# Gated linear attention and a maxout block on one core: a third unit in two-token rows, padded log sums without padding, and new due times in the kernel's planner

## Chip, cores and metric

One Trainium2 chip, one core. The metric is the device time of one execution in microseconds (us), the median over several runs. Lower is better.

## What is computed

For each of 4 batches and 8 heads a recurrent state of 48 x 48 is decayed and updated over 768 tokens, and read out by q. The result (3072 tokens x 384 features) goes through two projections whose maximum is projected back.

```python
for t in range(S):                                   # q, k, v, alpha: (4, 8, 768, 48)
    state = alpha[:, :, t, :, None] * state + einsum('bhd,bhe->bhde', k[:, :, t], v[:, :, t])
    y[:, :, t] = einsum('bhd,bhde->bhe', q[:, :, t], state)
x = y.transpose(0, 2, 1, 3).reshape(B * S, H * D)    # 3072 x 384
out = maximum(x @ w1, x @ w2) @ w_out                # d_ff = 1024
```

## The kernel before, in words

**Units.** The work is cut into 12 units of 256 tokens: unit u is batch u % 4, token block u // 4. A unit has two chunks of 128 tokens. Each unit passes two stages, `gla(u)` (the recurrence, in chunk form) and `moe(u)` (the two projections and the output).

**The recurrence of a unit.** ACT takes the logarithm of alpha (`ln`, L463). PE sums the logarithms along the tokens with a triangular matrix (`sums`, `e_cs`: L474 or L480) and adds up the whole unit for the decay between chunks (L506). From unit 2 on (`PAIR`), POOL first adds the two halves into the tile `ls` (L498), and L506 works on that. ACT makes the exponentials (L511, L513, L516). POOL multiplies k (L552) and DVE q (L554) with them; PE transposes both (L562), DVE copies them out of PSUM (L565 or L570). PE makes the scores (L653), DVE masks them (L675), PE multiplies with v and the carried state (L684, L687), ACT copies the result (L695), PE transposes it (L701), DVE copies it (L706 or L710) into `xt`. The state goes through PE (L624, or L581), ACT or DVE (L636 to L640) and POOL (L605, L611).

**The projections of a unit.** The maximum is written as x w2 + relu(x (w1 - w2)), so the weights are prepared once: DVE makes `w12` = w1 - w2 (L442), PE, DVE and ACT make w2 w_out (L415 to L436), ACT or POOL cast w_out (L447). Per unit PE does h = x w12 (L741, four pieces of six matmuls), ACT or DVE the relu (L752, L749), PE the output product (L772: three matmuls on `w2o` and `xt`, eight on `wo` and `gt`, for each of two halves), ACT the copy (L780), and an ACT queue the store (L788).

**Two-token rows.** `TWO` lists the units whose q, k and v are loaded as rows of two neighbouring tokens (384 B per head and row) instead of one (192 B). alpha is always loaded so. Such a unit has three loads of 384 KB for q, k, v (L384); another has six of 192 KB (L398). In a unit of `TWO`, the sums use the whole PE array (`ti`, `ts`, L474); otherwise they use 64 rows of it (`t2`, L480), which the code calls tiled. `v` is brought into place by two POOL copies (L536) and two ACT copies (L540) instead of two POOL copies `vc` (L573), the state product is one L581 group of 16 matmuls instead of two L624 groups of 4, and L653 of either chunk needs the transposes of both.

**What sets the order.** All instructions are first listed with an engine, an assumed duration, an assumed latency to the reader, the tiles read and written, and a key. `Plan.schedule` then walks through time: each engine takes, of what is ready by the assumed times and has its PSUM banks, the step with the lowest key; after a tiled step on PE the `join` key counts instead, which for L480 is 10u - 5 and for L653 lower by 50. The order found is written out per engine; on the chip an engine runs its instructions in exactly that order and waits for what is late. `gla(u)` has keys 10u to about 10u + 5, `moe(u)` 10u + 20 to 10u + 26. `OFF0` adds 8.8 to the key of PE's output products of units 0 and 1 and -0.7 to that of POOL's `kn` (L552) there. Loads stand in SP's order; their assumed latency grows from 2.5 to 5.0 us (`LATE`) with the unit. Where the plan leaves PE idle in its first 40 us, `busy` puts matmuls on zeros (L453).

**Loads.** Seven buffers (`NLD`) take the units in turn; the weights first lie in buffers 4 to 6. `HEAD` is the order of the first loads: units 0 and 1 and the weights. Then unit 2 and so on follow.

Of the kernel before, what the change touches and what calls it, by code (L numbers as in the profile page):

```python
# [23 lines left out]
class Plan:  # L24
# [16 lines left out]
        self.psum.setdefault(name, [banks, group, 0, None])  # L41

    def add(self, eng, fn, dur, reads=(), writes=(), key=0.0, lat=None, ps=(), tiled=False, join=None):
        if self.u is not None and writes and isinstance(writes[0], tuple):
            d = (self.off0 if self.u < 2 else self.off).get(f"{eng}:{writes[0][0]}", 0)
            key, join = key + d, None if join is None else join + d
        o = Op(len(self.ops), eng, fn, dur, self.LAT[eng] + self.PAD if lat is None else lat, key)
        o.tiled, o.join = tiled, key if join is None else join
        for r in reads:
            if r in self.last_w:  # L50
                o.deps.add(self.last_w[r])
            self.readers.setdefault(r, []).append(o.n)
        for w in writes:
            if w in self.last_w:
                o.deps.add(self.last_w[w])
            for r in self.readers.pop(w, ()):
                if r != o.n:
                    o.deps.add(r)
            self.last_w[w] = o.n
        for x in (*reads, *writes, *ps):  # L60
            if x in self.psum and x not in o.ps:
                o.ps.append(x)
                self.psum[x][2] += 1
        o.w = (*writes, *reads)[:1]
        self.ops.append(o)
        return o
# [127 lines left out]
RELU_DVE = 1  # L194
TM_ACT = 1
X_LAST = 0
LATE = 2.5
KEY_T2 = 17
TWO = (0, 1)
MERGE = 3  # L200
COMBO = 99
JOIN_CS = -5
# [2 lines left out]
RING = 3  # L205
PAIR = 2
PAIR_ON = 'POOL'
OFF = {}
OFF0 = {'PE:op': 8.8, 'POOL:kn': -0.7}
HEAD = 'k0 a0 a1 q0 v0 k1 q1 w20 w22 w21 wo0 v1 wo1 wo2 wo3 w11 w10 w13 w12'  # L210


# [1 line left out]
def kernel(  # L214
# [75 lines left out]
        return t.rearrange("p (h r d) -> p r h d", r=2, h=H)  # L290

    P = Plan()
    P.off, P.off0, P.u = OFF, OFF0, None
    add = P.add

    def bank(x):
# [73 lines left out]
    for i in range(RING):  # L370
        add("DVE", lambda i=i: nc.vector.memset(KN[i], 0.0), 0.2, writes=[("kn", i)], key=-6)
        add("DVE", lambda i=i: nc.vector.memset(QN[i], 0.0), 0.2, writes=[("qn", i)], key=-5)
    for i in range(4):
        add("DVE", lambda i=i: nc.vector.memset(SB[i], 0.0), 0.2, writes=[("sb", i)], key=-4)


    def load(u, what="akqv"):
        n, (b, cp) = u % NLD, (u % B, u // B)
        t0 = 256 * cp
        lat = 2.5 + max(0.0, min(LATE, LATE * (u - 1) / 3.0))  # L380
        ws = [({4: "w2f", 5: "w1f", 6: "wof"}[u], g) for g in range(3 if u == 4 else 4)] if u in (4, 5, 6) else []

        def pairs(dst, src, keys):
            add("SP", lambda: nc.sync.dma_start(  # L384
                out=dst.rearrange("p (h x) -> p h x", h=H),
                in_=src[b, :, t0 : t0 + 256, :].rearrange("h (p r) d -> p h (r d)", r=2)),
                1.26 if u in TWO else 1.5, writes=[*keys, *ws], key=-1, lat=lat)

        if "a" in what:
            pairs(LD[n][:, 0, :], alpha, [("af", n)])  # L390
        rest = [x for x in (("k", "kf", KF, k), ("q", "qf", QF, q), ("v", "vf", VF, v)) if x[0] in what]
        if u in TWO:
            for _, nm, T, src in rest:
                pairs(T[n], src, [(nm, n, 0), (nm, n, 1)])
            return
        for a in range(2):
            for _, nm, T, src in rest:
                add("SP", lambda T=T, src=src, a=a: nc.sync.dma_start(  # L398
                    out=nat(T[n])[:, a],
                    in_=src[b, :, t0 + 128 * a : t0 + 128 * a + 128, :].rearrange("h p d -> p h d")),  # L400
                    0.99, writes=[(nm, n, a), *ws], key=-1, lat=lat)


    def load_w(m, g):
        fs = slice(256 * g, 256 * g + 256)
        if m == "2":
            dst, src, t = w2f[:, g, :], moe_w2[128 * g : 128 * g + 128, :], 1.36
        elif m == "1":
            dst, src, t = w1f[:, :, fs], moe_w1[:, fs].rearrange("(s p) f -> p s f", p=128), 1.15
        else:  # L410
            dst, src, t = wof[:, 2 * g : 2 * g + 2, :], moe_w_out[fs, :].rearrange("(s p) d -> p s d", p=128), 1.1
        add("SP", lambda: nc.sync.dma_start(out=dst, in_=src), t, writes=[(f"w{m}f", g)], key=-1, lat=2.5)

    def w2_rows(ds):
        add("ACT", lambda: nc.scalar.copy(out=w2h[:, ds, :], in_=w2f[:, ds, :]),  # L415
# [52 lines left out]

    def e_cs(u):
        lg = LG[u % 2]  # L470
        if u in TWO:
            for i in range(2):
                for r in range(2):
                    nc.tensor.matmul(csv(u, i), lhsT=ts if r > i else ti, rhs=lg[:, r, :, 0:D],  # L474
                                     start=(r == 0), stop=(r == 1))
            return
        for r in range(2):
            for a in range(2):
                s = slice(64 * a, 64 * a + 64)
                nc.tensor.matmul(csv(u, a), lhsT=t2[s, r, 128 * a : 128 * a + 128], rhs=lg[s, r, :, 0:D],  # L480
                                 start=(r == 0), stop=(r == 1))

    def sums(u):
        by2 = u in TWO
        add("PE", lambda: e_cs(u), 0.65 if by2 else 0.33, reads=[("lg", u % 2), "tt" if by2 else "t2"],
            writes=[("cs", u, 0), ("cs", u, 1)], key=10 * u + (0 if by2 else CS_UP), tiled=not by2, join=10 * u + (0 if by2 else JOIN_CS))

    def exps(u):
        lg, de, k0 = LG[u % 2], DE[u % 8], 10 * u
# [5 lines left out]
        ls = LS[u % 2]  # L495
        if pair:
            ns = nc.vector if PAIR_ON == "DVE" else nc.gpsimd
            add(PAIR_ON, lambda: ns.tensor_add(out=ls, in0=lg[:, 0], in1=lg[:, 1]),  # L498
                0.35 if PAIR_ON == "DVE" else 0.6, reads=[("lg", u % 2)], writes=[("ls", u % 2)], key=k0)

        def e_de():
            for j in range(HP):
# [16 lines left out]
    def gla(u):  # L519
# [10 lines left out]
        if by2:  # L530
            vx, qu = VX[TWO.index(u)], QU[TWO.index(u) % 2]
            vk = ("vx", u)
            v2 = two(VF[n])
            for a in range(2):
                s = slice(64 * a, 64 * a + 64)
                add("POOL", lambda a=a, s=s: nc.gpsimd.tensor_copy(out=vx[s, a : a + 2], in_=v2[s]),  # L536
                    0.9, reads=[("vf", n, a)], writes=[(vk, a)], key=k0 + 2.2)
            for a in range(2):
                o = slice(64 - 64 * a, 128 - 64 * a)
                add("ACT", lambda a=a, o=o: nc.scalar.copy(  # L540
                    out=vx[o, 2 * a], in_=v2[64 * a : 64 * a + 64, 1 - a]),
                    0.5, reads=[("vf", n, a)], writes=[(vk, 2 + a)], key=k0 + 2.5)

        def prep(i):
# [4 lines left out]
            qin = two(QF[n])[:, i] if by2 else nat(QF[n])[:, i]  # L549
            rk = [("kf", n, x) for x in ((0, 1) if by2 else (i,))]  # L550
            rq = [("qf", n, x) for x in ((0, 1) if by2 else (i,))]
            add("POOL", lambda: nc.gpsimd.tensor_mul(out=kn[:, :, 0:D], in0=kin, in1=EM[m3]),  # L552
                0.95, reads=[*rk, ("em", m3)], writes=[("kn", m3)], key=kk)
            add("DVE", lambda: nc.vector.tensor_mul(out=qn[:, :, 0:D], in0=qin, in1=csv(u, i)),  # L554
                0.5, reads=[*rq, ("cs", u, i)], writes=[("qn", m3)], key=kk)
            tp = ("tp", u, i)
# [7 lines left out]
            if by2:  # L564
                add("DVE", lambda: nc.vector.tensor_copy(  # L565
                    out=qu[:, :, :, :, i, :].rearrange("p a w j c -> p (w j) a c"),
                    in_=b16(tp, 1024).rearrange("p (y a c) -> p y a c", a=2, c=64)),
                    0.65, reads=[tp], writes=[("qu", u, i)], key=kk)
            else:
                add("DVE", lambda: nc.vector.tensor_copy(  # L570
                    out=QK[m3], in_=b16(tp, 1024).rearrange("p (w j c) -> p w j c", w=2, j=HP)),
                    0.6, reads=[tp], writes=[("qk", m3)], key=kk)
                add("POOL", lambda: nc.gpsimd.tensor_copy(out=VC[ci % 4], in_=nat(VF[n])[:, i]),  # L573
                    0.48, reads=[("vf", n, i)], writes=[("vc", ci % 4)], key=kk)
# [12 lines left out]
        def chunk(a):  # L587
# [6 lines left out]
                P.ps(x, 1, "g")  # L594
            if by2:
                qt = [qu[:, a, w].rearrange("p j r c -> p j (r c)") for w in range(2)]
                rqk, vc, rv, um, ru = [("qu", u, 0), ("qu", u, 1)], vx[:, 2 * a], [(vk, x) for x in range(4)], u2, "u2"
            else:
                qt = [QK[m3][:, w] for w in range(2)]
                rqk, vc, rv, um, ru = [("qk", m3)], VC[m4], [("vc", m4)], u16, "u16"  # L600
# [56 lines left out]
            elif a == 0:  # L657
                for x in (("pp", u, 1, 0), ("pp", u, 1, 1)):
                    P.ps(x, 1, "g")
                rd = [("qk", (2 * u + x) % RING) for x in range(2)]  # L660
                wr = [*pp, ("pp", u, 1, 0), ("pp", u, 1, 1)]
                if u >= COMBO and u + 1 < NU:
                    P.u = u + 1
# [198 lines left out]
```

## Time and profile before

| | |
|---|---|
| Time, median of 3 runs | 138.80 us (138.77 to 138.87) |
| The profiled execution | 139.23 us, its span 137.5 us |
| PE busy | 132.1 us (96%) |
| DVE, ACT, POOL busy | 95.6, 80.4, 77.3 us |
| L453 (matmuls on zeros) | 132 pieces, 11.0 us |
| L480 / L474 | 40 / 8 matmuls |
| L498 (POOL, `ls`) | 10 of 1153 ns |
| L536, L573 (POOL, v) | 4 of 820 ns, 20 of 502 ns |
| Loads L384 of k, q, v | 2 each, 384 KB |
| Loads L398 of k, q, v | 20 each, 192 KB |
| PE clock granted | full throughout |

The span is the time from the first to the last instruction of the profiled execution; its own time is 1.73 us longer, and the profiled execution is 0.43 us above the median of the runs. Durations below come from the profiled execution. PE is TensorE's matmuls, PEld its weight loads, DVE VectorE, ACT ScalarE, POOL GpSimd, SP SyncE; SPq and ACTq are DMA queues issued there. A matmul's own duration includes its pipeline, so the time between starts, or the rows of the chain of waits, tell what it costs PE.

### The profile page before, as it was taken

The numbers are of one execution on the slowest core, as the hardware profiler recorded it, in microseconds if no ns is written. First come the engines' busy times: TensorE is split into PE (matmuls) and PEld (weight loads), VectorE is DVE, ScalarE is ACT, GpSimd is POOL, SyncE is SP. The second block draws the span as 40 slices with busy tenths as digits, with TensorE's granted clock in tenths as the row PEclk, the third lists the DMA queues.
The fourth block names the chain that finished last, engine by engine and source line by source line (L and its number), as shares of the span: only waits on it lengthen the run. The fifth ranks groups of instructions, "written<-read, shape, count | busy, mean of one in ns | idle before, by whom it ended". The sixth has DMA issues, their size and how long they took to land.

```text
span 137.5 us, 4265 instructions
## 1 busy us (share of the span) xinstructions
PE 132.1 (96%) x1671; PEld 102.1 (74%) x1671; DVE 95.6 (70%) x202; ACT 80.4 (58%) x172; POOL 77.3 (56%) x138
## 2 busy tenths in 40 slices
PE   6999699999999999999999999999999999999991
PEld 6889586886667768777777877877777778787870
DVE  4948879953868967878977859858839748574300
ACT  3294790878355585575754944937837539245341
POOL 7469339317548548688685864973966928300000
PEclk9999999999999999999999999999999999999999
DMA  3999999899998997999999989999989630030213
GB/s 92 325 325 402 373 377 349 227 188 236 221 280 189 280 240 153 286 218 200 277 184 205 293 165 225 232 184 302 210 194 290 127 117 0 5 114 0 82 37 114
DMA packets 87428, 28.59 MB, mean 208 GB/s; under 512 B 81520, under 2 KB 86768, under 8 KB 87408
## 3 DMA queue, kind: packets, MB, share of 16 engines
q1 hardware_dynamic: 84240, 23.60, 72.8%
q10 hardware_dynamic: 3168, 4.72, 9.1%
q8 instruction: 13, 0.21, 0.6%
q14 instruction: 7, 0.06, 0.2%
HBM read 23.59 MB, written 4.72 MB: 206 GB/s over the span
## 4 chain that ended last, share of the span: by engine, by line
PE 85%; SPq 5%; DMA 5%; ACT 2%; issue 1%; ACTq 0%
PE pb L772 31%; PE pb L741 23%; PE pb L562 7%; SPq L384 5%; DMA ld<-in_moe_w_dram 5%; PE pb L653 5%; PE pb L687 3%; PE pb L432 3%; PE pb L701 3%; PE pb L684 3%; PE pb L480 3%; PE pb L624 2%; PE pb L506 1%; PE pb L422 1%; ACT w2h L415 1%
## 5 line engine op out<-in xcount | busy, mean ns | idle before, releaser
L772 PE MATMUL pb<-wo,gt 128*128 128x384 f16 (+2 forms) x200 | 38.9, 319 | 0.0
L552 POOL TENSOR_TENSOR kn<-ld,em 128x384 f16<-128x384 f32 x24 | 23.5, 998 | 21.4 <-ACT em L511 18.8
L741 PE MATMUL pb<-xt,w 128*128 128x256 f16 x288 | 35.4, 272 | 0.0
L675 DVE TENSOR_TENSOR pt<-pb,u 128x512 f16<-128x512 f32 x48 | 29.9, 683 | 0.9 <-PE pb L653 0.6
L741 PEld LDWEIGHTS <-w 128*128 128x128 f16 x288 | 27.0, 98 | 3.6
L752 ACT ACTIVATE gt<-pb 128x512 f16<-128x512 f32 x37 | 21.8, 604 | 11.8 <-PE pb L741 11.4
L611 POOL TENSOR_TENSOR sb<-tm,dd 64x192 f16<-64x192 f32 x40 | 20.8, 520 | 7.0 <-DVE tm L636 3.1
L780 ACT COPY os<-pb 128x384 f32<-128x384 f32 (+2 forms) x25 | 11.6, 468 | 19.8 <-PE pb L772 19.7
L772 PEld LDWEIGHTS <-gt 128*128 128x128 f16 x200 | 17.2, 97 | 7.6
L570 DVE COPY qk<-pb 128x1024 f16<-128x1024 f16 x20 | 13.7, 687 | 9.3 <-PE pb L562 6.1
L498 POOL TENSOR_TENSOR ls<-lg 128x512 f16<-128x512 f16 x10 | 11.5, 1153 | 8.8 <-ACT lg L463 8.3
L772 PE MATMUL pb<-w2o,xt 128*128 128x384 f16 (+2 forms) x75 | 15.8, 320 | 0.0
L511 ACT ACTIVATE em<-pb 128x384 f32<-128x384 f32 x24 | 10.8, 489 | 8.5 <-PE pb L480 8.5
L554 DVE TENSOR_TENSOR qn<-ld,pb 128x384 f16<-128x384 f32 x24 | 12.3, 549 | 4.5 <-ACT pb L513 3.9
L695 ACT CAST yc<-pb 128x384 f16<-128x384 f32 x24 | 11.9, 498 | 2.7 <-PE pb L687 2.7
L710 DVE COPY xt<-pb 128x384 f16<-128x384 f16 x20 | 7.1, 354 | 9.0 <-PE pb L701 6.9
L463 ACT ACTIVATE lg<-ld 128x768 f16<-128x768 f32 x12 | 10.3, 854 | 3.8 <-DMA ld<-in_alpha_dram 3.8
L749 DVE TENSOR_SCALAR gt<-pb 128x512 f16<-128x512 f32 x11 | 7.6, 692 | 6.7 <-PE pb L741 6.4
L453 PE MATMUL pb<-wsrc 128*128 128x128 f16 x132 | 11.0, 249 | 1.1 <-DVE wsrc L307 1.1
L636 DVE TENSOR_TENSOR tm<-pb,sb 64x192 f32<-64x192 f32 x32 | 11.3, 352 | 0.6
L687 PEld LDWEIGHTS <-pt 128*128 128x128 f16 x192 | 9.6, 96 | 1.9 <-DVE pt L675 0.3
L453 PEld LDWEIGHTS <-wsrc 128*128 128x128 f16 x132 | 9.8, 115 | 1.2 <-DVE wsrc L307 1.1
(81 smaller groups left out, 193.2 us busy)
## 6 DMA issues: line engine op xcount, KB each, us to landing
ld<-in_alpha_dram SPq DMA_DIRECT2D x12, 384.0 KB, 5.2
out_dram<-os ACTq DMA_DIRECT2D x11, 384.0 KB, 4.0
ld<-in_k_dram SPq DMA_DIRECT2D x20, 192.0 KB, 4.8
ld<-in_q_dram SPq DMA_DIRECT2D x20, 192.0 KB, 4.6
ld<-in_v_dram SPq DMA_DIRECT2D x20, 192.0 KB, 4.3
ld<-in_moe_w_dram SPq DMA_DIRECT2D x3, 512.0 KB, 6.7
ld<-in_moe_w_out_dram SPq DMA_DIRECT2D x4, 384.0 KB, 8.0
ld<-in_moe_w_dram SPq DMA_DIRECT2D x4, 384.0 KB, 8.0
```

The costliest lines, as they stand in the source:

```text
L453: nc.tensor.matmul(PB[b][:, 0:128], lhsT=wsrc, rhs=wsrc, start=True, stop=True)
L552: add("POOL", lambda: nc.gpsimd.tensor_mul(out=kn[:, :, 0:D], in0=kin, in1=EM[m3]), 0.95, reads=[*rk, ("em", m3)], writes=[("kn", m3)], ke ...
L554: add("DVE", lambda: nc.vector.tensor_mul(out=qn[:, :, 0:D], in0=qin, in1=csv(u, i)), 0.5, reads=[*rq, ("cs", u, i)], writes=[("qn", m3)], ...
L570: add("DVE", lambda: nc.vector.tensor_copy(out=QK[m3], in_=b16(tp, 1024).rearrange("p (w j c) -> p w j c", w=2, j=HP)), 0.6, reads=[tp], w ...
L611: add("POOL", lambda r=r, e=e: nc.gpsimd.tensor_mul(out=sb[r, :, e], in0=TM[tmo][r], in1=dd[r, :].unsqueeze(2).to_broadcast([64, HP, D])), ...
L675: add("DVE", lambda e=e: nc.vector.tensor_mul(out=pt[:, e], in0=b32(pp[e], 512).rearrange("p (j c) -> p j c", j=HP), in1=uv.unsqueeze(1).t ...
L687: nc.tensor.matmul(t[:, 96 * j + D * e : 96 * j + D * e + D], lhsT=pt[:, e, j, :], rhs=vc[:, 2 * j + e, :], start=not has, stop=(e == 1) o ...
L695: add("ACT", lambda: nc.scalar.copy(out=yc, in_=b32(yp, DM)), 0.38, reads=[yp], writes=[("yc", ci % 2)], key=kk)
L741: nc.tensor.matmul(t[:, m, :], lhsT=w12[:, ds, f * 128 : f * 128 + 128], rhs=xt[:, ds].rearrange("p a c -> p (a c)"), start=(ds == 0), sto ...
L752: add("ACT", lambda g2=g2, v2=v2: nc.scalar.activation(out=g2, in_=v2(), func=ACTF.Relu), 0.48, reads=[x], writes=[("gt", u % 3, f2)], key ...
L772: nc.tensor.matmul(b32(x, c1 - c0), lhsT=l, rhs=r, start=first and y == 0, stop=last and y == len(ws) - 1)
L780: add("ACT", lambda m=m, x=x, c0=c0, c1=c1: nc.scalar.copy(out=os_[:, m, c0:c1], in_=b32(x, c1 - c0)), 0.06 + w / 1200.0, reads=[x], write ...
```

## The change

- **Unit 2 joins `TWO`**, with a third pair of `VX` tiles and the two `QU` tiles used in turn; its output rows are stored accordingly.
- **`LATER`**: in the plan, loads of units above 4 get 0.6 us more latency for each unit (4.2 us for unit 11). Loads of w2 are planned with 3.1 instead of 2.5 us.
- **`ls` without padding**: L498 adds 48 of the 64 columns of each head; the rest of the tile is set to zero once by two DVE memsets. Its planned duration is 0.9 instead of 0.6 us.
- **Early sums in two groups**: in units of `TWO`, the sums of the second half and of the first are two steps with keys 10u - 1 and 10u instead of one.
- `OFF`, `OFF0` and their effect go; a table `PRI` takes their place and is empty. `KN_DVE` and `VX_DVE` could move steps to DVE and are empty. Planned durations of `kn` and `vx` become 0.97 and 0.87.

```diff
     def add(self, eng, fn, dur, reads=(), writes=(), key=0.0, lat=None, ps=(), tiled=False, join=None):
-        if self.u is not None and writes and isinstance(writes[0], tuple):
-            d = (self.off0 if self.u < 2 else self.off).get(f"{eng}:{writes[0][0]}", 0)
+        if writes:
+            x = writes[0] if isinstance(writes[0], tuple) else writes
+            d = self.pri.get(f"{eng}:{'.'.join(str(y) for y in x)}@{self.u}", 0)
             key, join = key + d, None if join is None else join + d
...
+LATER = 0.6
 LATE = 2.5
 KEY_T2 = 17
-TWO = (0, 1)
+TWO = (0, 1, 2)
...
-OFF = {}
-OFF0 = {'PE:op': 8.8, 'POOL:kn': -0.7}
+KN_DVE = ()
+VX_DVE = ()
+PRI = {}
...
-    P.off, P.off0, P.u = OFF, OFF0, None
+    P.pri, P.u = PRI, None
...
+    for i in range(2):
+        add("DVE", lambda i=i: nc.vector.memset(LS[i], 0.0), 0.2, writes=[("ls", i)], key=KEY_T2)
...
-        lat = 2.5 + max(0.0, min(LATE, LATE * (u - 1) / 3.0))
+        lat = 2.5 + max(0.0, min(LATE, LATE * (u - 1) / 3.0)) + LATER * max(0, u - 4)
...
-        add("SP", lambda: nc.sync.dma_start(out=dst, in_=src), t, writes=[(f"w{m}f", g)], key=-1, lat=2.5)
+        add("SP", lambda: nc.sync.dma_start(out=dst, in_=src), t, writes=[(f"w{m}f", g)], key=-1, lat=3.1 if m == "2" else 2.5)
...
     def e_cs(u):
         lg = LG[u % 2]
-        if u in TWO:
-            for i in range(2):
-                for r in range(2):
-                    nc.tensor.matmul(csv(u, i), lhsT=ts if r > i else ti, rhs=lg[:, r, :, 0:D],
-                                     start=(r == 0), stop=(r == 1))
-            return
...
     def sums(u):
-        by2 = u in TWO
-        add("PE", lambda: e_cs(u), 0.65 if by2 else 0.33, reads=[("lg", u % 2), "tt" if by2 else "t2"],
-            writes=[("cs", u, 0), ("cs", u, 1)], key=10 * u + (0 if by2 else CS_UP), tiled=not by2, join=10 * u + (0 if by2 else JOIN_CS))
+        if u not in TWO:
+            add("PE", lambda: e_cs(u), 0.33, reads=[("lg", u % 2), "t2"], writes=[("cs", u, 0), ("cs", u, 1)],
+                key=10 * u + CS_UP, tiled=True, join=10 * u + JOIN_CS)
+            return
+        for i in (1, 0):
+            def e_two(i=i):
+                for r in range(2):
+                    nc.tensor.matmul(csv(u, i), lhsT=ts if r > i else ti, rhs=LG[u % 2][:, r, :, 0:D],
+                                     start=(r == 0), stop=(r == 1))
+            add("PE", e_two, 0.325, reads=[("lg", u % 2), "tt"], writes=[("cs", u, i)], key=10 * u - i)
...
-            add(PAIR_ON, lambda: ns.tensor_add(out=ls, in0=lg[:, 0], in1=lg[:, 1]),
-                0.35 if PAIR_ON == "DVE" else 0.6, reads=[("lg", u % 2)], writes=[("ls", u % 2)], key=k0)
+            add(PAIR_ON, lambda: ns.tensor_add(out=ls[:, :, 0:D], in0=lg[:, 0, :, 0:D], in1=lg[:, 1, :, 0:D]),
+                0.42 if PAIR_ON == "DVE" else 0.9, reads=[("lg", u % 2)], writes=[("ls", u % 2)], key=k0)
...
-                    0.65, reads=[tp], writes=[("qu", u, i)], key=kk)
+                    0.65, reads=[tp], writes=[("qu", TWO.index(u) % 2, i)], key=kk)
...
-                rd = [("qk", (2 * u + x) % RING) for x in range(2)]
+                rd = rqk if by2 else [("qk", (2 * u + x) % RING) for x in range(2)]
```

Left out are the places where `KN_DVE` and `VX_DVE` choose an engine (both empty) and where readers of `qu` follow its new name.

More of the change, by code (lines that the diff above doesn't have):

```diff
@@ L535, in gla @@
                 s = slice(64 * a, 64 * a + 64)
-                add("POOL", lambda a=a, s=s: nc.gpsimd.tensor_copy(out=vx[s, a : a + 2], in_=v2[s]),
-                    0.9, reads=[("vf", n, a)], writes=[(vk, a)], key=k0 + 2.2)
+                on, ns = ("DVE", nc.vector) if 2 * u + a in VX_DVE else ("POOL", nc.gpsimd)
+                add(on, lambda a=a, s=s, ns=ns: ns.tensor_copy(out=vx[s, a : a + 2], in_=v2[s]),
+                    0.6 if on == "DVE" else 0.87, reads=[("vf", n, a)], writes=[(vk, a)], key=k0 + 2.2)
             for a in range(2):
@@ L551, in prep @@
             rq = [("qf", n, x) for x in ((0, 1) if by2 else (i,))]
-            add("POOL", lambda: nc.gpsimd.tensor_mul(out=kn[:, :, 0:D], in0=kin, in1=EM[m3]),
-                0.95, reads=[*rk, ("em", m3)], writes=[("kn", m3)], key=kk)
+            on, ns = ("DVE", nc.vector) if ci in KN_DVE else ("POOL", nc.gpsimd)
+            add(on, lambda: ns.tensor_mul(out=kn[:, :, 0:D], in0=kin, in1=EM[m3]),
+                0.55 if on == "DVE" else 0.97, reads=[*rk, ("em", m3)], writes=[("kn", m3)], key=kk)
             add("DVE", lambda: nc.vector.tensor_mul(out=qn[:, :, 0:D], in0=qin, in1=csv(u, i)),
@@ L596, in chunk @@
                 qt = [qu[:, a, w].rearrange("p j r c -> p j (r c)") for w in range(2)]
-                rqk, vc, rv, um, ru = [("qu", u, 0), ("qu", u, 1)], vx[:, 2 * a], [(vk, x) for x in range(4)], u2, "u2"
+                rqk, vc, rv, um, ru = [("qu", TWO.index(u) % 2, 0), ("qu", TWO.index(u) % 2, 1)], vx[:, 2 * a], [(vk, x) for x in range(4)], u2, "u2"
             else:
```

## Prediction

> **What bounds the kernel now.** I read the page first: engine shares, the 40 slices, and the chain that ended last.
>
> ```profile
> PE 132.1 (96%) x1671; PEld 102.1 (74%) x1671; DVE 95.6 (70%) x202; ACT 80.4 (58%) x172; POOL 77.3 (56%) x138
> PE   6999699999999999999999999999999999999991
> PE 85%; SPq 5%; DMA 5%; ACT 2%; issue 1%; ACTq 0%
> ```
>
> The reader is to see that PE is the last link for 85% of the span, and that the rest (SPq, DMA) lies at the start. So the second view was the chain in order of time, where each row is start, length, work:
>
> ```profile
> 20.87 0.43 PE pb L432 x2
> 21.30 0.39 PE pb L453 x7
> 21.69 0.45 PE pb L581 x16
> 22.14 3.03 PE pb L432 x18
> ```
>
> ```profile
> 31.32 0.43 PE pb L480 x4
> 31.75 0.19 PE pb L506 x4
> ...
> 36.93 0.33 PE pb L653 x8
> 37.26 0.59 PE pb L772 x3
> 37.85 0.33 PE pb L653 x8
> 38.18 1.08 PE pb L772 x6
> 39.26 0.43 PE pb L480 x4
> 40.00 0.08 PE pb L506 x4
> ...
> 46.07 0.55 PE pb L653 x16
> 46.62 1.42 PE pb L741 x12
> ...
> 57.01 0.55 PE pb L653 x16
> 57.57 0.33 PE pb L480 x4
> 57.89 0.19 PE pb L506 x4
> ```
>
> L453 is filler (matmuls on zeros). Its last row is at 21.30; from 22.14 to 133.98 the rows follow each other without a hole. The span is therefore "22.1 us until PE never lacks work, plus 111.9 us of PE work, plus 3.5 us of tail". A change matters only if it alters one of these: it starts the full stretch earlier, alters PE's own work, or opens a hole in it. The third view, the list of waits from 24 to 134 us, has only two kinds that name a load (L552 2.6 us once, L573 0.4 us once), and the windows there show PE 3.00 busy of 3.00 us. Loads do not hold PE up today, so earlier loads are worth nothing by themselves.
>
> The same rows price a change of tile shape. L480 and L653 use part of the 128x128 array. L653 x16 costs 0.55 us, in two pieces 0.33 + 0.33; L480 costs 0.43 alone and 0.33 straight behind L653. The piece that follows pays too: twelve L741 take 1.42 us at 46.62 against 1.31 us elsewhere, and L506 takes 0.19 behind L480 against 0.08 behind L687. So an entry costs 0.10 and an exit 0.11, and joining two such stretches saves 0.21 us.
>
> The fourth view, the timeline of ACT, shows when the logarithms that L480 needs are there:
>
> ```profile
> 37.34 0.85 ACT L463 ACTIVATE lg<-ld 128x768 f16<-128x768 f32 x1
> 45.77 0.83 ACT L463 ACTIVATE lg<-ld 128x768 f16<-128x768 f32 x1
> ```
>
> Unit 3's are ready at 38.19 when unit 2's last L653 ends at 38.18; unit 4's at 46.60 when unit 3's ends at 46.62. Both sums just miss the stretch they could have joined; unit 5's (57.57) is the first that is joined, and later ones are joined too.
>
> **The change, part by part (PE us, minus is faster).**
>
> *Loads of unit 2.* Three loads of 384 KB replace six of 192 KB. In the trace, loads in two-token rows of units 0 and 1 land 1.21 us apart (4.24, 5.45, 6.64, 7.85, 9.07, 10.28), which is 325 GB/s. Unit 2's six natural ones land from 28.91 to 33.30, its alpha at 28.15: 5.15 us for six, 0.86 each. Three two-token ones should take 3 x 1.21 = 3.63 us, so everything behind them on SP's queue can come 1.5 us earlier. Worth nothing alone, as said; it feeds the joins below.
>
> A rule speaks against this. The Trainium skill (DMA: Bandwidth & Descriptors, Specifications) asks for at least 512 B per transfer for line rate; rows of 192 B and 384 B both lie under it. Read as a step, it would give this edit nothing, and without the joins the sum would be +0.11 instead of -0.31, 138.9 us. The landings show 229 GB/s for 192 B rows and 325 GB/s for 384 B rows, so I go by them.
>
> *Sums of unit 2.* L474 replaces L480: in unit 0 its four matmuls run from 6.43 to 7.08, 0.65 us, on the whole array. Before: 0.43 + exit 0.11. So +0.11. The two groups order them finer; same matmuls, nothing.
>
> *Key-value product of unit 2.* One L581 x16 (0.45) replaces two L624 (0.17 each): +0.11 if it joins L653 as in unit 0 (12.10, then 12.55), +0.22 with an exit of its own as in unit 1 (the eighteen L432 behind it take 3.03 us where 18 x 0.162 is 2.92). I take +0.22: unit 2's v lands last, as unit 1's does.
>
> *L653 of unit 2.* Today two stretches, 0.33 + 0.33 and two exits of 0.11: 0.88. In two-token rows both need both transposes and come together: 0.55 + 0.11 = 0.66. So -0.22.
>
> *Joins.* With unit 3's and unit 4's alpha 1.5 us earlier, each of their sums can stand behind the L653 of the unit before. The planner picks a tiled piece first after a tiled piece (`JOIN_CS`, `JOIN_PP`), and it does so in every unit from 5 on. -0.21 each: from 0 (L653 moves up as far as the logarithms do) to -0.42. I take -0.42, as both missed by under 0.05 us.
>
> *Before 22 us.* The order of the first loads stays, so nothing lands earlier. The L432 x18 stretch waits for the casts L447 on POOL (21.21, 21.98, 22.75), which follow the copies L536 of unit 1's v, landed at 19.39. The new latency of w2 (3.1) and the split sums reorder ACT and PE before that. ACT today waits 2.6 us for w2 with the tm copies (L638) queued behind; if they go first, POOL's L611, DVE's L636 and PE's L684 behind them come up to 2.3 us sooner (L638 ran at 15.39, its input L581 ended at 13.05), but what is late next is again the 19.39 landing. Taken 0; from -0.2 (one 0.20 piece of L687 moved ahead of 22.1) to +0.3 (one 0.29 to 0.45 piece pushed behind).
>
> *Edits that I cost at nothing.* Two memsets of LS on DVE: 0.27 each by the kn memset (0.8 us for three), in DVE's 1.47 us wait before 8.74; uncovered, 0.54 of DVE before unit 0's qn. L498 on 384 instead of 512 elements: 1.153 x 0.75 = 0.86 us estimated, at most 1.00 by L552 with 384; ten times 0.15 to 0.29 us less on POOL, which waits 18.8 us for ACT before L552, so hidden. Unit 2's extra POOL (L536 2 x 0.82 for L573 2 x 0.50: +0.64) and ACT (two L540, +1.02): covered by the 1.5 us of the loads and POOL's idle 5.0 us before 30.34; what is queued behind them is unit 2's second kn on POOL and its yc on ACT, and uncovered they cost what the slower rival says. `LATER` moves the planned place of unit 11's loads by 4.2 less the gain; its logarithms run at 106.73 and its sums at 112.84, a lead of 6.1 us, so it is covered. The kn offset of -0.7 keeps kn before vx or behind it as it was.
>
> *OFF0 dropped.* The output products of units 0 and 1 (44 L772 of 0.162, 7.1 us) lose 8.8 of delay: they come earlier, the work is the same. Nothing, as long as PE finds other work later.
>
> Sum: +0.11 +0.22 -0.22 -0.42 = **-0.31 us**. The profiled execution took 139.23 us with a span of 137.5; by the sum 138.92 and 137.2. It was 0.43 above the median of the runs, 138.80, which I move by the same amount: **138.5 us**.
>
> **Rivals.**
>
> *The reserve runs dry (slower).* Unit 0's and 1's output products now come first, and nothing is kept for the wait on unit 2. Today the last of them ends at 42.75, unit 2's h (L741) starts at 44.59, and its input (L710) was ready at 43.32; unit 3's transposes, its L624 and a w2o piece (0.17 + 0.56 + 0.49 + 0.45 + L701 0.17 = 1.84 us) fill in. If the extra ACT and POOL work comes on the path (0.64 + 1.02), L710 is ready at 44.98. Unit 3's L653 and second transposes (key 34.5) now stand behind unit 1's output (34), so the filler can be late as well. PE would wait from 0.4 us (44.98 against 44.59) to 2.2 us (against 42.75): about 1.0, with +0.11 for unit 2 and no joins 139.9. It decides once L710 is ready later than 44.6. For it: PE's reserve there is under 2 us. Against: q, k, v land sooner, and unit 3's too.
>
> *Nothing moves (same).* Unit 3's and unit 4's L653 move up with their logarithms, the joins fall out: +0.11, or -0.10 with one join; 138.7 to 138.9. For it: PE is full anyway, and the whole stretch only changes its order. Against: both sums miss by almost nothing.
>
> **How the numbers follow.** This kernel's measurement tells 0.2%, 0.28 us, from no change: 138.52 to 139.08. Forecast 0.40 (137.9 to 138.5: both joins, perhaps a product that joins, -0.11, and up to -0.2 before 22 us). Same 0.29. Slower 0.31, 139.1 to 140.4, likeliest in its lower half, since a partial hole is likelier than the full one. The range 137.9 to 139.8 leaves the upper end of that rival and a little below. The likeliest case alone: 137.9 to 138.5.
>
> **What the profile will show.** Right: L480 in 36 pieces and L474 in 12; unit 3's and 4's L480 at 0.33 straight behind L653; alpha of unit 3 landing near 33.4 rather than 34.89; the last filler still at 21 to 22 us and no hole after it. Wrong: filler or waits of PE later than 22.5, PE waiting for L710 between 38 and 46 us, or holes behind 110 us, where late planned loads would have pushed unit 11.

## The result and the profile after

The changed kernel took 138.84 us (median of 6 runs, 138.80 to 139.25); the kernel before took 138.91 us beside it (6 runs). The ratio is 1.0000, 95% interval 0.9986 to 1.0015. So by time the case that came is the prediction's "nothing moves" (0.29), not its forecast of 138.5 us (0.40). The measured time lies in the stated range, but not for that case's reason: the joins came, and a longer end of the program took their gain back.

The page of the changed kernel, its three lines that answer to those shown before:

```profile
PE 130.8 (95%) x1671; PEld 101.5 (74%) x1671; DVE 95.7 (70%) x204; ACT 81.8 (60%) x174; POOL 75.0 (55%) x138
PE   6897999999999999999999999999999999999990
PE 84%; DMA 5%; SPq 4%; DVE 3%; issue 1%; ACT 0%; ACTq 0%; DVEq 0%
```

PE is still the last link, and the new piece is DVE with 3%. Line numbers have moved: L653 is now L661, L480 L479, L474 L490, L506 L512, L581 L589, L741 L749, L772 L780. The chain in order of time, start, length and work:

```profile
21.43 0.51 PE pb L589 x16
21.95 3.03 PE pb L437 x18
...
25.55 0.66 PE pb L749 x6
26.21 0.83 PE pb L749 x6
...
36.52 0.45 PE pb L589 x16
36.97 0.33 PE pb L479 x4
37.30 0.22 PE pb L661 x8
37.52 0.60 PE pb L780 x3
...
38.54 0.33 PE pb L661 x8
38.87 0.76 PE pb L780 x4
...
45.19 0.55 PE pb L661 x16
45.75 0.33 PE pb L479 x4
46.07 0.19 PE pb L512 x4
```

The reader is to see three things. Both sums (L479 of units 3 and 4) now cost 0.33 and stand behind another tiled piece, as forecast. Six L749 take 0.83 at 26.21 where six take 0.66 just before: PE waits 0.17 us there. And the full stretch begins at 21.95 against 22.14.

To compare kernels without the scatter of the first loads, I read four lengths from each profiled execution:

- **U**, from the landing of w1's first quarter to the end of PE's last matmul.
- **R**, from the start of the seventh matmul of unit 0's h (its second piece, behind the wait at 26.21) to the end of PE's last matmul. But for unit 2's own pieces it holds the same matmuls in every row with a number.
- **The tail**, from the landing of the last store to the end of the span.
- **Outside**, what the time of the profiled execution has beyond its span.

Each experiment has 12 runs, the change 6.

| kernel | median us | ratio to before, 95% | U us | R us | tail us | DMAs | outside us |
|---|---|---|---|---|---|---|---|
| before, profile shown first | | | 110.78 | 108.16 | 0.90 | 103 | 1.72 |
| ctl_before (before again) | 138.86 | 0.9991 (0.9977 to 1.0005) | 110.90 | 108.17 | 0.90 | 103 | 1.71 |
| **the change** | 138.84 | 1.0000 (0.9986 to 1.0015) | 110.53 | 107.74 | 1.10 | 100 | 1.71 |
| after_w2_25 | 139.01 | 1.0002 (0.9987 to 1.0017) | 110.41 | 107.73 | 1.10 | 100 | 2.06 |
| after_two01 | 139.56 | 1.0040 (1.0025 to 1.0055) | not read | not read | not read | 103 | not read |
| before_no_hold | 139.56 | 1.0044 (1.0027 to 1.0061) | 111.54 | 108.83 | 0.90 | 103 | 1.72 |
| after_104dma | 138.63 | 0.9973 (0.9952 to 0.9995) | 110.64 | 107.74 | 0.84 | 104 | 1.71 |
| before_108dma | 139.50 | 1.0037 (1.0019 to 1.0054) | 110.90 | 108.16 | 1.10 | 108 | 1.74 |
| after_sums1 | 139.18 | 1.0001 (0.9980 to 1.0022) | 110.77 | other order | 1.10 | 100 | 1.86 |
| after_later0 | 139.24 | 1.0024 (0.9997 to 1.0051) | 110.90 | 108.10 | 1.10 | 100 | 1.71 |
| before_unit2 | 139.50 | 1.0021 (0.9988 to 1.0054) | 110.85 | 108.05 | 1.10 | 100 | 2.05 |
| after_held | 139.52 | 1.0020 (0.9994 to 1.0046) | 110.89 | 107.95 | 1.10 | 100 | 2.07 |
| after_ls512 | 139.43 | 1.0017 (0.9993 to 1.0042) | 111.00 | 108.18 | 1.10 | 100 | 2.05 |
| after_w2_104dma | 138.84 | 0.9959 (0.9935 to 0.9983) | 110.41 | 107.73 | 0.84 | 104 | 2.08 |

Medians of different rows come from three sets of runs, in which the kernel before took 138.87 (rows 2, 4 to 6), 139.02 (rows 7 to 10) and 139.22 us (the last four); compare ratios. The profile of after_two01 is of an execution of 417 us: its lengths are not read, its order is.

*What U and R say.* Three traces with the order of before give U 110.78, 110.90, 110.90 (mean 110.86), two with the order of the changed kernel 110.53 and 110.64 (mean 110.59), two with w2 at 2.5 us 110.41 both. So the change takes about 0.27 us from U and adds 0.20 us to the tail: -0.07 us, which fits a ratio of 1.0000 within 0.2 us. R repeats to 0.01 us and is 0.42 shorter; 0.17 of that is lost just ahead of R, in the wait at 26.21. (In after_104dma that wait is 0.39, and its first h starts 0.11 sooner after the landing.)

*What "outside" says.* It belongs to the kernel, not to one execution: in every execution of the kernel before with its span on record it is 1.66 to 1.79 us (spans to 0.1 us), in every one of the five kernels with 2.05 to 2.08 it is 2.01 to 2.15; after_sums1 lies between, at 1.76 to 2.11. These 0.35 us are 0.25% of the time, more than the change takes from U, and no length within the span has them.

*What the ratios of the last four rows hold.* By their lengths (U, tail and outside) they should lie 0.2 to 0.3% higher than they do. The kernel before itself had longer spans in that set than in the first (median 137.4 against 137.1 us); why is not shown. So the last four rows are read by their lengths first.

### The profile page after: what moved, and what is told of

Read it like the earlier page. It is cut to its first block, busy times and chain, and to the rows that moved or that the text cites. A ratio compares the mean times of both kernels' runs of the same rounds, so it can differ in the third digit from the quotient of the medians.

```text
span 137.1 us, 4253 instructions
## 1 busy us (share of the span) xinstructions
PE 130.8 (95%) x1671; PEld 101.5 (74%) x1671; DVE 95.7 (70%) x204; ACT 81.8 (60%) x174; POOL 75.0 (55%) x138
## 4 chain that ended last, share of the span: by engine, by line
PE 84%; DMA 5%; SPq 4%; DVE 3%; issue 1%; ACT 0%; ACTq 0%; DVEq 0%
PE pb L780 31%; PE pb L749 23%; PE pb L570 7%; DMA ld<-in_q_dram 5%; PE pb L661 4%; SPq L389 4%; PE pb L695 4%; PE pb L709 3%; PE pb L692 3%; PE pb L437 2%; PE pb L479 2%; PE pb L632 2%; DVE w2T L431 1%; PE pb L512 1%; PE pb L589 1%
## 5 line engine op out<-in xcount | busy, mean ns | idle before, releaser
L780 PE MATMUL pb<-wo,gt 128*128 128x384 f16 (+2 forms) x200 | 39.5, 319 | 0.0
L749 PE MATMUL pb<-xt,w 128*128 128x256 f16 x288 | 35.7, 272 | 0.0
L749 PEld LDWEIGHTS <-w 128*128 128x128 f16 x288 | 26.7, 98 | 3.5 <-DVE w L447 0.3
L619 POOL TENSOR_TENSOR sb<-tm,dd 64x192 f16<-64x192 f32 x40 | 20.1, 502 | 8.2 <-DVE tm L644 5.2
L780 PEld LDWEIGHTS <-gt 128*128 128x128 f16 x200 | 17.2, 97 | 7.6
L578 DVE COPY qk<-pb 128x1024 f16<-128x1024 f16 x18 | 12.3, 686 | 12.0 <-PE pb L570 8.8
L562 DVE TENSOR_TENSOR qn<-ld,pb 128x384 f16<-128x384 f32 x24 | 12.4, 550 | 6.5 <-ACT pb L519 4.6
L780 PE MATMUL pb<-w2o,xt 128*128 128x384 f16 (+2 forms) x75 | 15.8, 320 | 0.0
L504 POOL TENSOR_TENSOR ls<-lg 128x384 f16<-128x384 f16 x10 | 9.1, 907 | 6.9 <-ACT lg L468 6.5
L644 DVE TENSOR_TENSOR tm<-pb,sb 64x192 f32<-64x192 f32 x32 | 11.2, 351 | 0.6
L458 PE MATMUL pb<-wsrc 128*128 128x128 f16 x124 | 10.2, 246 | 1.1 <-DVE wsrc L310 1.1
L718 DVE COPY xt<-pb 128x384 f16<-128x384 f16 x18 | 6.3, 351 | 6.5 <-PE pb L709 5.0
L519 ACT ACTIVATE pb<-pb 128x384 f32<-128x384 f32 x24 | 10.7, 481 | 0.0
```

What stands on the lines that cost most here:

```text
L578: add("DVE", lambda: nc.vector.tensor_copy(out=QK[m3], in_=b16(tp, 1024).rearrange("p (w j c) -> p w j c", w=2, j=HP)), 0.6, reads=[tp], w ...
L619: add("POOL", lambda r=r, e=e: nc.gpsimd.tensor_mul(out=sb[r, :, e], in0=TM[tmo][r], in1=dd[r, :].unsqueeze(2).to_broadcast([64, HP, D])), ...
L644: nc.vector.tensor_add(out=TM[tmi][r], in0=t[r, :, e], in1=sb[r, :, e])
L749: nc.tensor.matmul(t[:, m, :], lhsT=w12[:, ds, f * 128 : f * 128 + 128], rhs=xt[:, ds].rearrange("p a c -> p (a c)"), start=(ds == 0), sto ...
L780: nc.tensor.matmul(b32(x, c1 - c0), lhsT=l, rhs=r, start=first and y == 0, stop=last and y == len(ws) - 1)
```

## The experiments

**A control, and w2 planned at 2.5 us again.** At first the shorter stretch of PE could have been chance or could have been given back before 22 us. ctl_before is the kernel before without an edit. after_w2_25:

```diff
-... key=-1, lat=3.1 if m == "2" else 2.5)
+... key=-1, lat=2.5)
```

> The kernel before, unchanged, as a control for what one execution shows. Two numbers are read from each trace: S, the start of the eighteen w2*w_out matmuls from which PE no longer lacks work (before 22.14 us, after 21.95), and W, from S to PE's last matmul (before 111.84, after 111.40). Theory 1 (given back): the change took 0.44 us from W, and its new order before 22 us gave it back; then this execution has W 111.8 again, and S near 21.7 if its time is 138.8 us. Theory 2 (nothing moved): the shorter W is the spread of executions; then W here is as likely 111.4.

> The changed kernel with w2's loads planned at 2.5 us again. Theory 1: ACT again waits for w2 ahead of the tm copies, DVE's order before 22 us is that of before; S comes near 21.6 to 21.7, W stays 111.4, time 138.4 to 138.6 us. Theory 2: 138.8 us, S and W within 0.1 of the changed kernel's.

Measured: S came at 21.88 in the control, 21.88 in the changed kernel and 21.95 with w2 at 2.5 us, so theory 1's "given back before 22 us" falls: the start did not move. (S and W here are from the start of the matmuls and to the modelled end of the last; by that reading W is 112.47 and 112.33 for before, 112.07 for the change, 111.89 with w2 at 2.5.) Theory 2 falls too, since the shorter stretch stays; the control's U of 110.90 is above every trace of the changed order. What the w2 edit does cost is the 0.17 us at 26.21. The timelines of DVE show why, first of the changed kernel:

```profile
23.95 1.08 DVE L447 TENSOR_TENSOR w<-ld,ld 128x768 f16<-128x768 f32 x1
24.95 0.34 DVE L644 TENSOR_TENSOR tm<-pb,sb 64x192 f32<-64x192 f32 x1
25.22 1.81 DVE L447 TENSOR_TENSOR w<-ld,ld 128x768 f16<-128x768 f32 x2
```

and of after_w2_104dma, which has w2 at 2.5 us:

```profile
23.92 2.07 DVE L447 TENSOR_TENSOR w<-ld,ld 128x768 f16<-128x768 f32 x2 [0.16 <-DMA ld<-in_moe_w_dram]
25.92 0.34 DVE L644 TENSOR_TENSOR tm<-pb,sb 64x192 f32<-64x192 f32 x1
```

With w2 planned later, an L644 stands between the first two quarters of w12, and the second piece of unit 0's h waits for it. In the second kernel the chain has `25.57 1.31 PE pb L749 x12` in one piece. But after_w2_25 had the shorter span, 137.0 us, without a shorter time: it took 2.06 us outside the span where the control and the changed kernel took 1.7, and so did all its twelve executions (2.03 to 2.15). What that time is spent on, no run here shows.

**What holds the output products back.** The slower rival, tried in the kernel before, and unit 2's rows taken out of the changed kernel:

```diff
-OFF0 = {'PE:op': 8.8, 'POOL:kn': -0.7}
+OFF0 = {}
```
```diff
-TWO = (0, 1, 2)
+TWO = (0, 1)
```

> The kernel before without the 8.8 of delay on the output products of units 0 and 1 (and the -0.7 on kn). The slower rival of the prediction: PE runs out of work between 38 and 55 us, 0.4 to 1.2 us, time 139.2 to 140.0 us. If the reserve is not needed: within 0.2 us of before.

> The changed kernel with unit 2 in natural rows again, all else as changed. Theory 1: unit 3's and 4's sums stand alone again (+0.42 in W), and with the output products of units 0 and 1 not held back PE runs out of work once between 38 and 55 us by 0.3 to 1.0 us: W 112.2 to 112.9, time 139.5 to 140.2 us. Theory 2: unit 2's rows do nothing, 138.8 us.

Both cost 0.4% (ratios 1.0044 and 1.0040). For before_no_hold the trace shows the rival's mechanism; its place was wrong. The list of PE's waits between 24 and 134 us of before_no_hold has one row (waits in us, times, longest), and the timeline puts it at 53, not 43 us:

```profile
PE pb L741 <- DVE xt L710: 0.3, 1, 0.3
```
```profile
52.63 0.65 PE L772 MATMUL pb<-w2o,xt 128*128 128x384 f16 x3
53.58 1.14 PE L741 MATMUL pb<-xt,w 128*128 128x256 f16 x9 [0.29 <-DVE xt L710]
```

Three L772 at 0.162 end at 53.12 and L741 starts at 53.58: 0.46 us of hole, before unit 3's h. The rest of the 0.67 us in R is one more entry into the tiled shape (15 after 22 us instead of 14, 0.21 us by the chain's rows). In the changed kernel no such hole appears. Unit 2's rows are therefore worth 0.4% where the products are not held back: they pay for the dropped delay rather than add to a gain. How is only in part shown. In the order of after_two01, as in before_no_hold, PE enters the tiled shape 15 times after its first h (11 in the changed kernel), unit 4's sum is joined and those of units 3 and 5 stand alone, against the expected 3 and 4. Whether it has the hole too can't be read.

**The end of the program.** The tail was 0.20 us longer with the change, always by the same amount. In the trace, SP ends the program by waiting for eight DMA semaphores in a fixed order: five waits, for the fourth with the third, the fifth with the second, the sixth with the first, the seventh, the eighth. With nothing left to wait for they start 0.065 us apart (136.03, 136.10, 136.17, 136.23, 136.29 in the changed kernel). DMAs take these semaphores in turn. With 103 DMAs the last store has the seventh, and one wait follows its own; with 100 it has the fourth, the first to be waited for, and four follow. The list of SP's waits shows it: in the kernel before (control) the stores are waited for four times, most of it long before the end; in the changed kernel once.

```profile
SPq L857 <- DMA out_dram<-os: 30.6, 4, 25.9
```
```profile
SPq L865 <- DMA out_dram<-os: 31.0, 1, 31.0
```

To test it, four (or, in the kernel before, five) stores are issued in two halves; PE's order stays:

```diff
+def e_st():
+    if u in (5, 6, 7, 8):                        # before_108dma: (4, 5, 6, 7, 8)
+        for m in range(2):
+            nc.scalar.dma_start(out=out[r0 + 128 * m : r0 + 128 * m + 128, :], in_=os_[:, m, :])
+        return
+    ...                                          # the one store as it was
```

> The changed kernel with the stores of units 5 to 8 split in two halves of 192 KB each: 104 DMAs instead of 100 (before has 103), PE's order untouched. Theory 3 (epilogue): the DMAs take eight semaphores in turn, and at the end SP waits for these in a fixed order, 0.065 us each; with 100 DMAs the last store's semaphore is the fourth of eight, so four more waits follow its landing, with 103 the seventh and one more. The time from the last landing to the end of the span was 0.90 to 0.91 us in the kernel before and 1.11 in the changed one. With 104 it is the eighth: 0.84 to 0.91 us, and 138.5 to 138.65 us. Theory 2 (nothing moved, the tail is chance): 138.8 us.

> The kernel before with the stores of units 4 to 8 split in two halves: 108 DMAs. Theory 3: the last store's semaphore is the fourth of eight, 1.11 us from the last landing to the end, 139.0 to 139.1 us. Theory 2: 0.90 us and 138.85 us.

The tails came out as written: 0.84 us with 104 DMAs (eighth), 1.10 with 108 (fourth). So the length of the tail is shown, with both signs. The times went the same way, 0.27% faster and 0.37% slower than the kernel before. For after_104dma that fits: 0.22 us less U and 0.06 less tail are 0.20%. For before_108dma the tail alone makes 0.14%, and the lower end of its interval is 0.19%: U and R are those of before, and the rest is not in its trace, whose span (137.5 us) is below the median of its executions (137.8).

**The other parts, each undone alone.** The early sums in one step, no growing margin, the delays back, the padded log sums back:

```diff
-        for i in (1, 0):
-            def e_two(i=i): ...              # two steps, keys 10u - 1 and 10u
+        def e_two(): ...                     # all four matmuls, one step, key 10u
```
```diff
-LATER = 0.6
+LATER = 0.0
```
```diff
-            d = self.pri.get(...)
+            d = (self.off0 if self.u < 2 else {}).get(f"{eng}:{writes[0][0]}", 0)   # 'PE:op': 8.8, 'POOL:kn': -0.7
```
```diff
-            add(PAIR_ON, lambda: ns.tensor_add(out=ls[:, :, 0:D], ...), ... 0.9, ...)
+            add(PAIR_ON, lambda: ns.tensor_add(out=ls, in0=lg[:, 0], in1=lg[:, 1]), ... 0.6, ...)
```

> The changed kernel with the early sums in one step per unit again. If the split only orders the same matmuls finer (the prediction), it is worth nothing: 138.85 us, W within 0.1 of 112.1. If unit 2's way to its h hangs on it, now that the output products are not held back, PE runs out of work once near 43 us by 0.3 to 0.6 us: W 112.4 to 112.7, 139.1 to 139.4 us.

> The changed kernel without the growing margin (LATER = 0). The prediction: nothing, the logarithms run 3 to 6 us ahead of their sums in the late units: 138.85 us, W within 0.1 of 112.1, no load named among PE's waits. If the margin is needed, an engine waits for a late load behind 60 us and PE has a hole there: W over 112.4, 139.1 us or more.

> The changed kernel with OFF0's delays back. The prediction says that holding the output products is order alone: 110.5 to 110.7 us from w1's first landing to PE's end, 138.85 us. If the delay is still worth the half microsecond that it was worth in the kernel before: 110.0 us and 138.3 us.

> The changed kernel with the log sums over 512 padded elements again, planned at 0.6 us, without the two memsets. The prediction: POOL gets 10 x 0.25 us more and PE nothing, 138.85 us. If the wrong due time of this step (0.6 planned, 1.15 measured) misplaces the small matmuls that wait for it: unit 3's sum is parted from the tiled stretch beside it, +0.2 to +0.4 us of PE, 139.0 to 139.2 us.

By time none is clear of no change against the kernel before: the intervals of after_later0, after_held and after_ls512 begin just below 1, that of after_sums1 lies around it. So what follows rests on one trace each. U rises from 110.59 to 110.77, 110.90, 110.89 and 111.00, but U of one order differs by 0.1 us, so R and the stretches in the tiled shape tell more:

- *Early sums in one step:* 12 stretches instead of 11; from the first h to PE's end 108.68 us, against 108.38 in after_w2_25, which like this run has no wait at 26. That is 0.30, of which one stretch makes 0.21.
- *No margin:* R 0.36 longer, by one wait (below).
- *Delays back:* R 0.21 longer, by one stretch, as unit 2's product stands apart from unit 3's sum. But the wait at 26.21 is gone, so from the first h to PE's end it is 108.60 against 108.56: nothing. The rest of its U lies ahead of the first h, where one trace can't tell it from scatter.
- *Padded sums:* R 0.44 longer, by two stretches.

Without the margin, PE waits for a cast of ACT (0.34 us at 106.6 in the starts of its matmuls; its list of waits names 0.2 of it), with no load among PE's waits: the margin works through the order on ACT, not by covering a load that PE would wait for. With the padded sums, both joins are gone, though the loads are those of the changed kernel. The chain of after_ls512 (L659 scores, L477 sums, L510 the small ones):

```profile
36.89 0.55 PE pb L659 x16
...
38.36 0.43 PE pb L477 x4
38.80 0.18 PE pb L510 x4
...
45.24 0.55 PE pb L659 x16
45.79 0.76 PE pb L747 x6
46.55 0.43 PE pb L477 x4
46.98 0.19 PE pb L510 x4
```

0.43 twice where the changed kernel has 0.33, each with its own exit: R is 0.44 us longer, about two joins at 0.21. The join is worth what the prediction said, and it hangs on the `ls` edit, not on the loads alone. The likely part is the planned 0.9 us of that POOL step, since it sets the order; this run takes the narrower sum and the two memsets back with it, so that is not shown apart.

**Unit 2 alone, in the kernel before.** `TWO = (0, 1, 2)` and the tiles it needs, nothing else.

> The kernel before with unit 2 in two-token rows alone; the delays of the output products, w2 at 2.5, the early sums in one step, padded log sums and the old margin stay. By the terms of the prediction: unit 2's own PE work 0 to +0.1, unit 4's sum joins (-0.21), unit 3's perhaps: from w1's first landing to PE's end 110.5 to 110.7 us (before 110.8 to 110.9), the end 1.10 us after the last landing instead of 0.90 (100 DMAs): 138.8 to 139.0 us. If unit 2's rows did all the good: 110.4 us and 138.75.

Unit 4's sum is joined (0.33 at 45.96 behind 0.55), unit 3's is not (0.43 at 38.12), and unit 2's product (L586 in this kernel) stands alone. U is 110.85, as before and above the expected 110.5 to 110.7; R, which repeats better, is 0.11 shorter. That is the prediction's price: +0.11 +0.22 -0.22 for unit 2 and -0.21 for one join make -0.10. Against it stand 0.20 us of tail and 0.34 outside the span. So unit 2's rows by themselves bring PE 0.1 us and the program nothing.

**Both short ones together.** w2 at 2.5 us and 104 DMAs.

> The changed kernel with w2 planned at 2.5 us again and with 104 DMAs (stores of units 5 to 8 in halves): the two edits whose traces were shortest, together. Theory 3: from the last landing to the end 0.84 us; from the first landing of w1 to PE's end 110.4 us as with w2 at 2.5 alone (110.5 to 110.6 with 3.1); span 136.7 to 136.8, 138.45 to 138.6 us. If the 0.3 us that the w2 edit alone showed outside its span come back: 138.7 to 138.8 us.

Ratio 0.9959 (0.9935 to 0.9983): faster than the kernel before beside it, by 0.4%, with U 110.41, tail 0.84 and span 136.7 us. Its profiled execution again had 2.08 us outside the span, and by its lengths it should lead by 0.15 us, 0.1%; the rest is not explained, as for the other rows of its set. Its lead over after_104dma (0.9973) is within the intervals, so either may be the best version.

## Why the prediction was right, and where it was not

**PE's own work: right.** The sum said -0.31. By the chain's rows of the changed kernel unit 2's sums, product and scores and the two joins make: sums 0.65 against 0.54; product and scores 0.45 + 0.22 + 0.11 + 0.44 = 1.22 against 0.34 + 0.88 = 1.22; joins 2 x -0.21. That is +0.11, 0, -0.42: -0.31. The way differed, since unit 2's two score pieces did not come together; the first joined the product and unit 3's sum in one stretch (36.52 to 37.52). In the kernel before eight L562 took 0.56 at 43.09 where eight take 0.45, so 0.11 us of hole was there, against the prediction's "without a hole"; it is gone. -0.31 - 0.11 = -0.42 is what R measures.

**Before 22 us: taken 0, and right.** S is 21.88 in the control and in the changed kernel (22.09 in the profile shown first). But the new place of w2 left its mark later: 0.17 us at 26.21, inside the +0.3 that was allowed. -0.42 + 0.17 = -0.25; by U -0.27.

**The step that failed: "plus 3.5 us of tail".** The sum held the tail fixed. It grew by 0.20 us because three loads fewer moved the last store to another of eight semaphores. So the "same" case came without its own reason, that the joins fall out; that the tail took back just what they gave is luck. In the prediction's terms -0.31 should have stood with +0.20, at -0.11 us, 138.7: in the "same" case. The parts on the edits costed at nothing counted only what the removed loads did on the queues, not what their number does at the end.

**Joins: right in size, wrong in cause.** The text put them on alpha landing 1.5 us earlier. Unit 3's alpha landed at 32.56 instead of 35.08 in the control, 2.5 us earlier, but the same loads with the padded sums (after_ls512) gave no join, and before_unit2 only one. Unit 4's sum is joined in before_no_hold as well, with the loads of before. Unit 3's shares a stretch with unit 2's product only where unit 2's rows and the new `ls` are in and the delay is out. The joins came from the planned order of all these together.

**The Trainium skill's rule on transfers under 512 B (DMA: Bandwidth & Descriptors, Specifications).** Rows of 384 B landed k, q and v of unit 2 from 28.89 to 31.32, 1.21 us apart, again 325 GB/s. The measurement decides: the step from 192 to 384 B pays in landing times, though both lie under 512 B. The rule's forecast of 138.9 us came nearer to the time than 138.5, for another reason.

**What the profile was to show.** L480's 36 and L474's 12 matmuls, and both 0.33 pieces: seen. The last filler came at 18.8, not 21 to 22 us, and PE waited 0.3 us for DVE (L714) before its L589 at 21.43 instead; the L437 stretch started no earlier for it.

## What to carry to other kernels

When one engine is full, price a change by what that engine executes and by every length outside its full stretch, the end of the program too: here three DMAs fewer cost 0.20 us there. An edit to a hidden step can still cost the full engine, because its planned duration places that engine's steps. Compare by a length that repeats: one start point scattered by 0.1 us and hid a gain of 0.1, another repeated to 0.01. Undo each part alone before calling it idle: loads and held products each looked free, and each was worth 0.4% where the other was missing.

## What the runs showed of the hardware that was not expected

SP's five waits for eight DMA semaphores at the end follow one another 0.065 us apart, so the tail from the last landing was 0.84, 0.90 or 1.10 us in thirteen traces, by the number of DMAs alone (104; 103; 100 and 108). Time outside the span was the same in all executions of a kernel but differed between kernels that do nearly the same: 1.7 us in most, 2.05 to 2.08 in five, in between in one; what it is spent on is not in the trace.
